# A fused attention, MoE and gated layer in fp32 on one core: attention's small products gathered into one burst per run, and the gated layer's splits planned by when their loads land

## The chip, the cores and the metric

The kernel runs on one core of a Trainium2 chip. The metric is the device time of one execution in microseconds, as the median of several runs. Before the change it is 764.74 us (three runs, 764.42 to 764.76).

## What is computed

Three layers follow each other on 4 sequences of 576 tokens with 512 features, all in float32: attention over a window of 128 tokens with a linear bias per head, a two-layer MoE block with a norm ahead of it, and a gated layer that mixes along the sequence.

```python
scores = scale * np.matmul(q, k.transpose(0, 1, 3, 2))          # 4 x 8 heads, 576 x 576, 64 deep
mask = (rel >= 0) & (rel < window)
scores = np.where(mask, scores + bias[None], -1000000000.0)
attn = np.exp(scores - max); attn = attn / (sum + 1e-09)
x = attn @ v
...
xn = (x - mu) / np.sqrt(var + 1e-06) * g_ln
x = x + np.maximum(xn @ w_ch1, 0.0) @ w_ch2                      # 512 -> 2048 -> 512
...
h = gelu(x @ w_in); u, v = halves of h                           # 512 -> 2 x 512
v_n = (v - mu) / np.sqrt(var + 1e-06) * g_ln
v_s = np.einsum('ts,bsd->btd', w_sg, v_n) + b_sg[None, :, None]  # 576 x 576 along the sequence
out = x + (u * v_s) @ w_out
```

## The kernel before

Every large product is made of three products of float32 values cut into a high and a low part (high x high, high x low, low x high); the parts are made on the chip. A weight comes as 64-bit words by DMA into a buffer `st`, is rounded into a tile `sc` in five steps (Split64, lines 61 to 89: `first` on ACT, L72; `bits` 0 to 3 on DVE, L77, L79, L81, L84; `last` on ACT and POOL, L88 and L89), and gives a high part (as `wvh`) and a low part (`wvl`).

The program has two phases. The first, `phase1`, computes attention and the MoE interleaved. Attention is cut into 40 runs (L252 on): 32 wide ones of two units (128 query tokens of one pair of heads each) and 8 tail runs of one unit. A run goes through these steps: the scores on PE (`scores`, L408, products L444, in tail runs L430); for each of its units, in `unit` (L465), the mask and the reduction on DVE (L477 to L489), the exponential on ACT (L495), the sums and their reciprocals on DVE (L498, L499), the normalising on POOL, ACT or DVE (L503), a pair of transposes on PE (L513, into `tps`), and the copy with its mask (L527 to L533, with POOL's `sel`, L453); then the values on PE (`values`, L563, products L580) and their eviction on ACT (L557 to L560) into the tiles `x`. A group is 256 tokens; `norm(g)` (L594) starts a group's norm when all its runs are evicted: mean (sums on POOL L606, L608, product L611), squares on ACT (L644), their sums on POOL (L649, L651), the variance product (L659), the power on POOL (L665) and the product that spreads rstd (L669). The MoE (`moe`, L704) takes groups and eighths of the weights in a fixed order, `stream`. A step is two halves of 12 products of 128x256 with K = 128: `m1` (L743, into `ps_h`) or `m2` (L754, into `acc`); between them stand the relu on ACT (`hh`, L682) and its low half on DVE (`hl`, L684), and behind a group's last step `evac` (L687) with `et` and `x`.

The order of the instructions is set at build time by a planner (`Sched`). Each step is a generator that yields `Op(engine, estimated ns, priority, need=..., slots=..., token=...)`: it is started on its engine when the tokens in `need` are there and a slot is free, the earliest start first and then the lowest priority. Only the order on each engine comes from this; at run time engines wait for semaphores. An `Op` with engine None waits for its needs and takes no engine. `pts` and `tau` (L292 to L299) turn a unit's number into its priority, so that attention is spread over the MoE's steps; a norm's priority comes from `start` and `LBACK`.

When attention is over, `end_attention` (L801) spawns for each of 21 loads of the gated layer a `flow` (L934): one load on SP into one of four buffers `st` (NS2), and the split steps on ACT, DVE and POOL with three tiles `sc` (NC2). The loads are four pieces each of wv and wu (from `in_wi`), two of x, five of ws and four of wo. `open_1`, `open_2` and `open_3` (L890 to L908) make the room for their results when the MoE's last group is through its steps 7, 5 and 3; `open_2` also loads the bias `bb` and the gain `g` and scales both on DVE (L903). The second phase, `Phase2.run`, is the gated layer: v products (L994), u (L1070), the products along the sequence (L1087) and out (L1115), with the gelu in `ge` (L1026 to L1028) and `vg` (L1031).

## Time and profile before

| | |
|---|---|
| median of three runs | 764.74 us |
| the profiled execution | 765.15 us |
| its span in the profile | 763.4 us |
| mean granted clock of TensorE | 0.991 of full |
| busy: PE / DVE / ACT / POOL | 746.2 / 444.7 / 311.7 / 256.6 us |
| share of the span: PE / DVE / ACT / POOL | 98% / 58% / 41% / 34% |
| products L743 and L754 | 6 groups of 576, 160.7 to 166.7 us busy each |
| moved by DMA | 63.42 MB, 83 GB/s |

The span is what the hardware profiler covers, from the first to the last instruction; the execution's own time is 1.75 us longer. Matmuls overlap in the pipeline, so the durations of single products (0.28 us) add up to more than the time that passes; what a product takes of PE's time is read from the distance of two starts. Line numbers are those of the kernel before, unless a text says "of the changed kernel", where the code stands some 40 lines lower.

### The profile page before, as it was taken

The page shows a single profiled execution, that of the slowest core. Times are in us where ns is not written, and L with a number is a line of the kernel's source. Part 1 is how long each engine was busy: PE and PEld are TensorE (multiplying, and loading weights), DVE is VectorE, ACT ScalarE, POOL GpSimd, SP SyncE. Part 2 cuts the span into 40 slices and gives each one's busy share as a digit, 9 for nine tenths or more (in the row PEclk, how much of TensorE's full clock was granted, in tenths as well). Part 3 has the DMA queues.
Part 4 walks back from the last instruction along what each step waited for, and adds up shares of the span by engine and source line. Part 5 has one row for each costly group of instructions (what it writes and reads, how often), then busy time and mean ns, then how long its engine had stood idle before and what let it go on. Part 6 is the DMA issues. An engine that isn't in the chain of part 4 may idle for free.

```text
span 763.4 us, 15899 instructions
## 1 busy us (share of the span) xinstructions
PE 746.2 (98%) x6270; PEld 692.8 (91%) x6270; DVE 444.7 (58%) x1129; ACT 311.7 (41%) x805; POOL 256.6 (34%) x327
## 2 busy tenths in 40 slices
PE   7999999999999999999999999999899999999998
PEld 3669899999999999999999898999789999999997
DVE  6899888784542532443433335835776646656732
ACT  5896744432432522423423534232354333333410
POOL 2533423432421421412312323217255406317220
PEclk9999999999999999999999999999899999999999
DMA  9654621420121110111111324406130050160002
GB/s 304 203 174 134 179 83 30 131 70 22 59 95 29 49 57 21 44 56 56 29 43 43 79 83 157 142 29 178 38 124 1 32 169 1 47 203 0 2 32 93
DMA packets 51626, 63.42 MB, mean 83 GB/s; under 512 B 10336, under 2 KB 38880, under 8 KB 51552
## 3 DMA queue, kind: packets, MB, share of 16 engines
q1 hardware_dynamic: 51552, 62.41, 26.2%
q8 instruction: 49, 0.80, 0.5%
q14 instruction: 25, 0.20, 0.1%
HBM read 52.96 MB, written 9.44 MB: 82 GB/s over the span
## 4 chain that ended last, share of the span: by engine, by line
PE 90%; POOL 3%; DMA 2%; ACT 2%; DVE 2%; issue 1%; SPq 0%; DVEq 0%; POOLq 0%; ACTq 0%
PE acc L754 25%; PE ps_h L743 24%; PE ps_s L1087 8%; PE ps_u L1070 7%; PE ps_o L1115 7%; PE ps_v L994 6%; PE o L580 4%; PE s L444 3%; PE tps L513 2%; PE ps_ln L659 1%; DMA st<-in_wo 1%; PE ps_ln L602 1%; DMA st<-in_w 1%; POOL x2l L986 1%; PE ps_w L352 1%
## 5 line engine op out<-in xcount | busy, mean ns | idle before, releaser
L754 PE MATMUL acc<-hh,w2h 128*128 128x256 f32 x576 | 166.0, 288 | 2.0 <-ACT hh L682 2.0
L743 PE MATMUL ps_h<-xh,w1h 128*128 128x256 f32 x576 | 166.7, 289 | 0.0
L754 PE MATMUL acc<-hl,w2h 128*128 128x256 f32 x576 | 162.4, 282 | 0.5 <-DVE hl L684 0.5
L754 PE MATMUL acc<-hh,w2l 128*128 128x256 f32 x576 | 162.2, 282 | 0.0
L743 PE MATMUL ps_h<-xh,w1l 128*128 128x256 f32 x576 | 160.7, 279 | 0.0
L743 PE MATMUL ps_h<-xl,w1h 128*128 128x256 f32 x576 | 160.7, 279 | 0.0
L684 DVE SCALAR_TENSOR_TENSOR hl<-ps_h,hh 128x512 fp32r<-128x512 f32 x72 | 49.6, 689 | 141.0 <-ACT hh L682 140.7
L754 PEld LDWEIGHTS acc<-hh,w2h 128*128 128x128 f32 x576 | 110.0, 191 | 6.8 <-ACT hh L682 3.3
L743 PEld LDWEIGHTS ps_h<-xh,w1h 128*128 128x128 f32 x576 | 108.5, 188 | 3.0 <-issue 2.8
L754 PEld LDWEIGHTS acc<-hh,w2l 128*128 128x128 f32 x576 | 110.9, 192 | 0.0
L754 PEld LDWEIGHTS acc<-hl,w2h 128*128 128x128 f32 x576 | 110.1, 191 | 0.8 <-DVE hl L684 0.8
L743 PEld LDWEIGHTS ps_h<-xh,w1l 128*128 128x128 f32 x576 | 108.9, 189 | 0.0
L743 PEld LDWEIGHTS ps_h<-xl,w1h 128*128 128x128 f32 x576 | 108.4, 188 | 0.1
L453 POOL TENSOR_SCALAR_AFFINE_SELECT m<-m 128x256 f32<-128x256 f32 x118 | 53.1, 452 | 154.5 <-ACT m L530 151.2
L682 ACT ACTIVATE hh<-ps_h 128x512 fp32r<-128x512 f32 x72 | 42.8, 594 | 95.5 <-PE ps_h L743 95.5
L495 ACT ACTIVATE t<-t,sm 128x128 f32<-128x128 f32 x144 | 56.2, 393 | 29.5 <-DVE sm L489 29.5
L503 POOL TENSOR_TENSOR t<-t,sm 128x256 f32<-128x256 f32 x52 | 32.9, 634 | 90.0 <-DVE sm L499 70.5
L530 ACT ACTIVATE m<-tps 128x256 f32<-128x256 f32 x62 | 23.7, 382 | 85.2 <-PE tps L513 84.8
L986 POOL TENSOR_TENSOR gl<-gt,gh 128x576 fp32r<-128x576 f32 x16 | 22.9, 1430 | 53.3 <-ACT gh L985 53.3
L72 ACT ACTIVATE sc<-st 128x512 f32<-128x512 f32 (+1 forms) x52 | 30.7, 598 | 24.5 <-DMA st<-in_wo 6.1
L1028 ACT ACTIVATE ge<-ge 128x512 f32<-128x512 f32 (+1 forms) x34 | 22.4, 658 | 37.1 <-DVE ge L1027 37.1
L81 DVE SCALAR_TENSOR_TENSOR sc<-st,sc 128x512 int32<-128x512 int32 (+1 forms) x52 | 36.0, 696 | 0.4
(163 smaller groups left out, 1543.4 us busy)
## 6 DMA issues: line engine op xcount, KB each, us to landing
st<-in_w SPq DMA_DIRECT2D x24, 512.0 KB, 4.0
x2d<-x SPq DMA_DIRECT2D x18, 256.0 KB, 2.0
out<-xr SPq DMA_DIRECT2D x15, 288.0 KB, 2.1
st<-in_w SPq DMA_DIRECT2D x16, 256.0 KB, 2.7
st<-in_wi SPq DMA_DIRECT2D x8, 512.0 KB, 4.0
st<-x2d SPq DMA_DIRECT2D x8, 512.0 KB, 4.8
xr<-x2d SPq DMA_DIRECT2D x8, 512.0 KB, 6.6
rq<-in_q SPq DMA_DIRECT2D x28, 128.0 KB, 2.1
```

The costliest lines, as they stand in the source:

```text
L81: dve.scalar_tensor_tensor(out=xi, in0=self.wh, scalar=-0x40000000, in1=xi, op0=ALU.bitwise_and, op1=ALU.bitwise_or)
L453: pool.affine_select(out=out, in_=in_, pattern=pat, compare_op=ALU.is_ge, fill=0.0, base=-1 if up else 0, channel_multiplier=1 if up else -1)
L495: act.activation(out=t[:, h], in_=t[:, h], func=ACTF.Exp, bias=st[:, h:h + 1], scale=-1.0, accum_out=sums[:, h, 0:1])
L503: pool.tensor_tensor(out=t, in0=t, op=ALU.mult, in1=st[:, 6:8].rearrange("p (h o) -> p h o", o=1).to_broadcast([128, 2, 128]))
L682: act.activation(out=h, in_=ps, func=ACTF.Relu)
L684: dve.scalar_tensor_tensor(out=l, in0=ps, scalar=0.0, in1=h.bitcast(F32), op0=ALU.max, op1=ALU.subtract)
L743: pe.matmul(ps[:, half], w[:, kc, f], m[:, kc], start=kc == 0 and x == 0, stop=kc == 3 and x == 2)
L754: pe.matmul(accs[half][:, d], w[:, f, ds], m[:, k], start=fi and d == 0 and k == 0 and x == 0, stop=la and k == 1 and x == 2, skip_group_c ...
L994: self.nc.tensor.matmul(ps, xs[s][:, kc, c0:c0 + 128], self.wv[m][:, kc], start=kc == 0 and x == 0, stop=kc == 3 and x == 2)
L1070: pe.matmul(ps[:, z, 0:288], wu[s][:, kc, ds], self.x[m][:, kc, 288 * z:288 * z + 288], start=kc == 0 and x == 0, stop=kc == 3 and x == 2)
L1087: pe.matmul(ps[:, z, 0:288], l, r[:, 288 * z:288 * z + 288], start=n == 0, stop=n == len(mm) - 1)
L1115: pe.matmul(ps[:, z, 0:288], wo[s][:, kc, ds], gated[b][m][:, kc, 288 * z:288 * z + 288], start=n == 0, stop=n == 11)
```

## The change

From run KB = 13 on, scores, values and transposes are no longer three kinds of steps of their own. A new generator, `burst(n)`, is one step on PE: the scores of run n+1, the values of run n-1, and the transposes of all units of run n, in this order. It needs the normalised scores of run n (`nm`), the copies of the transposes before (`bl`), and everything that the values of run n-1 wait for (`R`). `scores(n)` returns without doing anything for n > 13, its products having moved into `quarters`; in `unit` the steps for the transposes and the values become steps without an engine that wait for the tokens which the burst sets. So the values of a run come one run later than before. There are 27 bursts (n = 13 to 39); the values of the last run stay a step of their own.

BB = (11, 6) moves the points of `pts`: attention runs four units earlier against the norms, and the last of the points lies 6 halves earlier. In the gated layer's `flow`, the first split step (ACT) now also needs the token `ld2` of its load, which the planner sets at the time when it estimates the load to have landed; the estimate of the first DVE step goes from 1100 to 680 ns, and DVE's steps of a flow count as users of the port that DVE and POOL share in the planner. No operation's shape changes.

```diff
--- before.py
+++ after.py
@@ -54,6 +54,10 @@
 WEARLY = {0: -990, 1: -989, 2: -898, 3: -897}
 NWARM, FILL = 14, 495
 ABANK = 1, 3, 5
+
+
+KB = 13
+BB = 11, 6
 
 NLO = 6
 
@@ -292,7 +296,7 @@
 
     pts = list(PACE)
     for g in range(NF, G):
-        pts.append((71 if g == 8 else 8 * g + 7, start[g] - LBACK[g == 8] - OC - 1))
+        pts.append((71 if g == 8 else 8 * g + BB[0], start[g] - LBACK[g == 8] - OC - 1 - (BB[1] if g == 8 else 0)))
 
     def tau(n):
         for (n0, t0), (n1, t1) in zip(pts, pts[1:]):
@@ -409,6 +413,8 @@
 
 
         p, tail, n = s.p, s.tail, s.n
+        if n > KB:
+            return
         if s.wide:
             z = min(y for _, y, _ in LW if y > p)
             nd = [("wq", z), ("wk", z)]
@@ -417,6 +423,10 @@
         sl = [("a%d" % h, 1, ("cp", n)) for h in range(2)] if n in ABANK else [("s", 1, ("cp", n))]
         yield Op("PE", 420 if tail else 700 if s.i0 == 0 else 810, s.tau, token=("A1", n), slots=sl,
                  need=nd + ([("A1", n - 1)] if n else []))
+        quarters(s)
+
+    def quarters(s):
+        p, tail, n = s.p, s.tail, s.n
         if n in ABANK:
             s.S = [ps_a.tile([128, 2, 256], F32, tag="a%d" % h, name="sa") for h in range(2)]
             s.parts = [(h, s.S[h]) for h in range(2)]
@@ -506,11 +516,14 @@
             for h in range(2):
                 scaled(o.eng, t[:, h], t[:, h], st[:, 6 + h:7 + h])
 
-        yield Op("PE", 220, pri + OB, token=("T", un),
-                 need=["cst", "unf"] + ([("bl", un - 2)] if un >= 2 else []) + ([("T", un - 1)] if un else []))
+        e.t = t
         tp = tps[:, un % 2]
-        for h in range(2):
-            pe.transpose(tp[:, h], t[:, h], ident)
+        if n >= KB:
+            yield Op(None, 0, pri, need=[("T", un)])
+        else:
+            yield Op("PE", 220, pri + OB, token=("T", un),
+                     need=["cst", "unf"] + ([("bl", un - 2)] if un >= 2 else []) + ([("T", un - 1)] if un else []))
+            transposed(e)
         new = ([(i - 1, 0)] if i == s.i0 and i > 0 else []) + [(i, int(not e.last))]
         o = Op(None, 0, pri, slots=[("m%d" % f, NM[f], ("C", n)) for j, f in new], token=("bl", un),
                need=[("bl", un - 1)] if un else [], alt=[("ACT", 275, 740)] + ([] if tail else [("DVE", 670 if i else 335, DVEX)]))
@@ -541,9 +554,13 @@
             nd.append(("wv", s.p))
         else:
             nd.append(("lv", n))
-        yield Op("PE", 500 if tail else 1020 if i > 1 else 760, pri + OC, need=nd, slots=[("o", 1, ("ev", n))],
-                 token=("C", n))
-        values(s)
+        if KB <= n + 1 < len(runs):
+            yield Op(None, 0, pri, need=nd, token=("R", n))
+            yield Op(None, 0, pri, need=[("C", n)])
+        else:
+            yield Op("PE", 500 if tail else 1020 if i > 1 else 760, pri + OC, need=nd, slots=[("o", 1, ("ev", n))],
+                     token=("C", n))
+            values(s)
         x = s.x()
         sl = []
         if x not in xt:
@@ -559,6 +576,31 @@
         else:
             act.activation(out=x[:, p, :], in_=s.O, func=ACTF.Copy)
         yield Op(None, 0, 0, token=("ev", n))
+
+    def transposed(e):
+        for h in range(2):
+            pe.transpose(tps[:, e.un % 2, h], e.t[:, h], ident)
+
+    def burst(s):
+        n = s.n
+        after = runs[n + 1] if n + 1 < len(runs) else None
+        nd = [("nm", e.un) for e in s.units] + [("bl", e.un - 2) for e in s.units if e.un - 2 < s.units[0].un]
+        nd += [("R", n - 1), "cst", "unf"] + ([("A1", n)] if n == KB else [])
+        sl = [("o", 1, ("ev", n - 1))]
+        if after:
+            nd += [("lq", n + 1), ("lk", n + 1)]
+            sl.append(("s", 1, ("cp", n + 1)))
+        dur = 300 + 140 * len(s.units) + (400 if runs[n - 1].tail else 820 if runs[n - 1].i0 else 600)
+        if after:
+            dur += 420 if after.tail else 850 if after.i0 else 600
+        yield Op("PE", dur, (after or s).tau, need=nd, slots=sl)
+        if after:
+            quarters(after)
+        values(runs[n - 1])
+        for e in s.units:
+            transposed(e)
+        for z in [("A1", n + 1), ("C", n - 1)] + [("T", e.un) for e in s.units]:
+            sched.done[z] = sched.free["PE"] + HOPP
 
     def values(s):
 
@@ -817,7 +859,7 @@
     for gen in ([warm(), constants()] + [load_wide(slice(x, y), t) for x, y, t in LW]
                 + [moe(), open_split(), last_quarter(), end_attention()]
                 + [weights(n) for n in range(40)] + [norm(g) for g in range(G)]
-                + [load(s) for s in runs if not s.wide] + [scores(s) for s in runs] + [unit(e) for e in units]):
+                + [load(s) for s in runs if not s.wide] + [scores(s) for s in runs] + [burst(s) for s in runs if s.n >= KB] + [unit(e) for e in units]):
         sched.spawn(gen)
     sched.run("end")
     for p in (ps_a, ps_h, wps.pop(), np_, cp):
@@ -940,14 +982,15 @@
         self.loaded.append(j)
         if j.shape:
             w = int(np.prod(j.shape))
-            yield Op("ACT", 190 + .833 * w, 10 ** 6 + n, need=[("p2", j.name)])
+            yield Op("ACT", 190 + .833 * w, 10 ** 6 + n, need=[("p2", j.name), ("ld2", n)])
             self.loaded.remove(j)
             j.step()
             self.todo[j.label] -= 1
             yield Op("POOL", 60 + 2.3 * w, 10 ** 6 + n, token=("st2", n))
             return
-        for k, (eng, dur) in enumerate((("ACT", 565), ("DVE", 1100), ("DVE", 602), ("DVE", 602), ("ACT", 530))):
-            yield Op(eng, dur, 10 ** 6 + n, need=[("p2", j.name)] if k == 4 else [],
+        for k, (eng, dur) in enumerate((("ACT", 565), ("DVE", 680), ("DVE", 602), ("DVE", 602), ("ACT", 530))):
+            yield Op(eng, dur, 10 ** 6 + n, port=eng == "DVE",
+                     need=[("ld2", n)] if k == 0 else [("p2", j.name)] if k == 4 else [],
                      slots=[("sc2", NC2, ("sc2", n))] if k == 0 else [],
                      token=("st2", n) if k == 3 else None)
             if k == 0:
```

On PE, in the middle of the MoE, where a wide run's unit is transposed; `ps_h<-` is a layer product, `tps<-ident,t` a transpose, `s<-` scores and `o<-` values. Before, a pair of transposes stands alone, and a little later scores and values together:

```order
L743 MATMUL ps_h<-xl,w1h_108 128x256
L743 MATMUL ps_h<-xh,w1l_109 128x256
L513 MATMUL tps<-ident,t 128x128 x2
L743 MATMUL ps_h<-xh,w1h_108 128x256
L743 MATMUL ps_h<-xl,w1h_108 128x256
...
L743 MATMUL ps_h<-xh,w1l_109 128x256
L444 MATMUL s<-rk,rq 64x192 x8
L580 MATMUL o<-m,rv 64x256 x2
L580 MATMUL o<-m,rv 64x128 x2
L754 MATMUL acc<-hh,w2h_110 128x256
```

With the change the same stretch holds one burst:

```order
L785 MATMUL ps_h<-xh,w1l_109 128x256
L454 MATMUL s<-rk,rq 64x64 x2
L454 MATMUL s<-rk,rq 64x128 x2
L454 MATMUL s<-rk,rq 64x192 x4
L622 MATMUL o<-m,rv 64x256 x2
L622 MATMUL o<-m,rv 64x128 x2
L582 MATMUL tps<-ident,t 128x128 x4
L796 MATMUL acc<-hh,w2h_110 128x256
```

The two pairs of a run's transposes have moved behind its neighbours' scores and values, and layer products follow behind the burst.

On POOL, at the last norm of the MoE and the first splits of the gated layer (`sq` the sums of squares, `var` the power, `wvl` a split's low part). Before:

```order
L649 TENSOR_TENSOR sq<-sq 128x512
L89 TENSOR_TENSOR wvl<-sc,wvh 128x512 x2
L651 TENSOR_TENSOR sq<-sq 128x256
L89 TENSOR_TENSOR wvl<-sc,wvh 128x512
L665 TENSOR_TENSOR var<-var,mh 128x2
L89 TENSOR_TENSOR wvl<-sc,wvh 128x512
```

With the change:

```order
L691 TENSOR_TENSOR sq<-sq 128x512
L693 TENSOR_TENSOR sq<-sq 128x256
L93 TENSOR_TENSOR wvl<-sc,wvh 128x512
L707 TENSOR_TENSOR var<-var,mh 128x2
L93 TENSOR_TENSOR wvl<-sc,wvh 128x512 x3
```

Two splits have moved from between the two sums to behind them, one of them behind the power.

On DVE, with the change, where the last group's relu (`hl`) meets the gated layer's splits (`sc`), and at the first v products. `bb` and `g` stand ahead of the last step (L88) of a split, and split steps stand between `et`, `x`, `ge` and `vg`:

```order
L85 SCALAR_TENSOR_TENSOR sc<-st,sc 128x512
L726 SCALAR_TENSOR_TENSOR hl<-ps_h,hh 128x512
L945 TENSOR_SCALAR bb<-bb 128x576
L945 TENSOR_SCALAR g_6797<-g_6797 128x4
L88 SCALAR_TENSOR_TENSOR sc<-st,sc 128x512
L726 SCALAR_TENSOR_TENSOR hl<-ps_h,hh 128x512 x2
...
L735 TENSOR_TENSOR et<-acc,rstd 128x512
L88 SCALAR_TENSOR_TENSOR sc<-st,sc 128x512
L739 TENSOR_TENSOR x<-x,et 128x512
L85 SCALAR_TENSOR_TENSOR sc<-st,sc 128x512
L1070 SCALAR_TENSOR_TENSOR ge<-ge,ps_v 128x512
L88 SCALAR_TENSOR_TENSOR sc<-st,sc 128x512
L1074 SCALAR_TENSOR_TENSOR vg<-ge,ps_v 128x512
```

Before, both steps L81 and L84 of that split stood ahead of `bb`, and no step of a split stood between `ge` and `vg`:

```order
L81 SCALAR_TENSOR_TENSOR sc<-st,sc 128x512
L84 SCALAR_TENSOR_TENSOR sc<-st,sc 128x512
L684 SCALAR_TENSOR_TENSOR hl<-ps_h,hh 128x512
L903 TENSOR_SCALAR bb<-bb 128x576
L903 TENSOR_SCALAR g_6814<-g_6814 128x4
L684 SCALAR_TENSOR_TENSOR hl<-ps_h,hh 128x512
```

The scaling of `bb` has moved from behind a finished split into the middle of one.

## Rows read from the trace of the kernel before

**Rows 1.** Page, chain that ended last, by engine
```profile
PE 90%; POOL 3%; DMA 2%; ACT 2%; DVE 2%; issue 1%; SPq 0%; DVEq 0%; POOLq 0%; ACTq 0%
```

**Rows 2.** Timeline of PE, a lone pair of transposes: start, us, what
```profile
152.11 0.28 PE L754 MATMUL acc<-hh,w2l 128*128 128x256 f32 x1
152.23 0.38 PE L513 MATMUL tps<-ident,t 128*128 128x128 f32 x2
...
152.57 0.28 PE L754 MATMUL acc<-hl,w2h 128*128 128x256 f32 x1
```

**Rows 3.** Timeline of PE, the scores of a run alone
```profile
207.26 0.28 PE L743 MATMUL ps_h<-xh,w1l 128*128 128x256 f32 x1
...
208.40 0.28 PE L754 MATMUL acc<-hl,w2h 128*128 128x256 f32 x1
```

**Rows 4.** Timeline of PE, the values of a run alone
```profile
87.03 0.28 PE L754 MATMUL acc<-hh,w2l 128*128 128x256 f32 x1
...
88.26 0.28 PE L743 MATMUL ps_h<-xl,w1h 128*128 128x256 f32 x1
```

**Rows 5.** Timeline of PE, scores and values in one break
```profile
221.31 0.28 PE L743 MATMUL ps_h<-xh,w1l 128*128 128x256 f32 x1
221.52 0.77 PE L444 MATMUL s<-rk,rq 64*64 64x64 f32 x16
...
223.24 0.28 PE L754 MATMUL acc<-hl,w2h 128*128 128x256 f32 x1
```

**Rows 6.** Timeline of PE, scores, values and a pair of transposes in one break
```profile
75.52 0.28 PE L754 MATMUL acc<-hh,w2l 128*128 128x256 f32 x1
...
77.24 0.44 PE L513 MATMUL tps<-ident,t 128*128 128x128 f32 x2
...
77.63 0.28 PE L754 MATMUL acc<-hl,w2h 128*128 128x256 f32 x1
```

**Rows 7.** The chain in order of time, 300 to 315 us: start, us, what
```profile
302.37 1.42 PE ps_h L743 x12
...
311.83 2.72 PE acc L754 x24
```

**Rows 8.** Timelines of POOL and PE, first long wait: [idle before <-releaser]
```profile
473.95 3.17 POOL L89 TENSOR_TENSOR wvl<-sc,wvh 128x512 fp32r<-128x512 f32 x2
477.08 0.90 POOL L651 TENSOR_TENSOR sq<-sq 128x256 f32<-128x256 f32 x1
...
478.04 0.61 PE L659 MATMUL ps_ln<-ones,sq 128*128 128x1 f32 x4 [2.29 <-POOL sq L651]
```

**Rows 9.** Three stretches: us, busy PE, PEld, DVE, ACT, POOL, granted clock, DMA, GB/s
```profile
478.50:482.90 4.40, 4.40 (x26) 4.40 (x26) 4.34 (x9) 2.39 (x4) 1.87 (x2) 0.61 0.36 119
538.20:543.30 5.10, 5.04 (x23) 5.04 (x24) 4.65 (x6) 0.94 (x2) 2.19 (x2) 0.50 0.00 0
551.90:556.20 4.30, 3.00 (x13) 2.18 (x12) 3.34 (x8) 2.00 (x5) 0.55 (x1) 1.00 0.77 253
```

**Rows 10.** Timeline of PE at the second long wait
```profile
537.31 0.43 PE L754 MATMUL acc<-hh,w2h 128*128 128x256 f32 x1 [1.99 <-ACT hh L682]
538.26 0.58 PE L754 MATMUL acc<-hl,w2h 128*128 128x256 f32 x1 [0.52 <-DVE hl L684]
```

**Rows 11.** Timeline of DVE, and the chain, before the second long wait
```profile
526.00 0.85 DVE L903 TENSOR_SCALAR bb<-bb 128x576 f32<-128x576 f32 x1 [2.41 <-DMA bb<-in_bsg]
...
528.18 6.56 DMA st<-in_wo
```

**Rows 12.** Timeline of PE, third v product of the gated layer
```profile
553.60 0.50 PE L994 MATMUL ps_v<-wvh,x2h 128*128 128x512 f32 x1 [1.30 <-DVE vg L1031]
```

**Rows 13.** Page, costliest groups: busy, mean ns, idle before, releaser
```profile
L81 DVE SCALAR_TENSOR_TENSOR sc<-st,sc 128x512 int32<-128x512 int32 (+1 forms) x52 | 36.0, 696 | 0.4
```

**Rows 14.** Timelines of PE and POOL, one tail unit from scores to normalised scores
```profile
438.36 0.56 PE L430 MATMUL s<-rk,rq 64*64 64x192 f32 x8
...
441.06 0.61 POOL L503 TENSOR_TENSOR t<-t,sm 128x256 f32<-128x256 f32 x1 [3.91 <-DVE sm L499]
```

## The prediction

> **What bounds the kernel now.** I read the page first, then the chain of waits, the timeline of PE at every place where the stream of layer products is interrupted, and last the busy times by stretch. Products with 256 columns of the MoE layer (L743, L754) are called layer products here. The chain is 90% PE [rows 1]: nearly everything counts that shortens PE's own stream, and nothing that only shortens another engine, unless PE waits for it. The reader is to see three kinds of lost PE time. The first is the breaks: each time attention puts a few small products into the stream, the stream needs some time beyond its own. The second is the pace of the layer products behind a break. The third is two long waits near the end of the MoE, each with a stretch of half clock behind it.
>
> A break is priced from the start of the last layer product ahead of it to the start of the second one behind it, less two steps of 0.113 us. A lone pair of transposes: 152.57 - 152.11 = 0.46, so 0.23 us [rows 2]. The scores of a run alone: 1.14 - 0.23 = 0.91 [rows 3]. Its values alone: 1.23 - 0.23 = 1.00 [rows 4]. Scores and values in one break: 1.93 - 0.23 = 1.70, which is 0.21 less than apart [rows 5]. Scores, values and a pair of transposes together: 2.11 - 0.23 = 1.88, so the pair costs 0.17 there instead of 0.23 [rows 6].
>
> The pace is the odd reading. The chain shows 12 layer products in 1.42 us, 0.118 each, and elsewhere 24 in 2.72 us, 0.113 each [rows 7]. Over the chain from 100 to 476 us about 1,450 of some 2,640 layer products go at the slower pace: 1,450 x 0.0047 = 6.8 us. The pace changes only at a break. Of 41 lone pairs of transposes 39 left the slow pace behind them; breaks of scores with values, and all 12 pairs that stood behind other small products, left the fast one.
>
> The first long wait: POOL does two splits (L89) of 3.17 us together, and only then the second sum of squares that the last norm needs, so PE idles 2.29 us ahead of the variance products [rows 8]. In the 4.40 us behind it the granted clock is 0.61 [rows 9], a mixture of the two levels: 4.40 x 0.39 = 1.7 us lost. The second: PE idles 1.99 us for the relu on ACT and 0.52 for its low half on DVE [rows 10], and 5.10 us then run at 0.50, which is 1.2 GHz [rows 9]: 2.55 lost. What made relu late is DVE: the scaling of bb stood in its queue and waited 2.41 us for its load [rows 11], and everything behind it slid.
>
> **The change, part by part.**
>
> A, the breaks. From product 252 of the stream on, the changed order has 48 breaks where there were 86. Of the 40 runs 12 already had scores and values joined; 6 more are joined now: 6 x 0.21 = 1.2 us. In 19 wide runs the pairs of transposes move from breaks of their own to the end of a burst, 0.23 to 0.17: with two pairs in a row, some of them already behind other products, I take 0.07 a run, 1.3 us. The tail runs and norms give some 0.2. Together -2.7; from 0 (the small products cost the same wherever they stand) to -4.0 (all 38 saved breaks at 0.11).
>
> B, the pace. In the changed order lone pairs are gone from run 13 on, every burst ends in transposes behind values, and the breaks that stay alone are a norm's mean, variance and rstd. I count the layer products behind such a break up to the next burst: 96 in each of four groups, some 130 in the last, about 520, and some 260 before the first burst as now. That makes 780 slow products, 3.7 us, where there were 6.8: **-3.1**. The ends are -6.8 (all fast) and +4.7 (a burst leaves the slow pace behind it, then all behind the first burst are slow, some 2,190, and the 260 ahead of it: 2,450 x 0.0047 = 11.5, less 6.8). I take the first value, since the nearest case [rows 6] left the fast pace behind its transposes.
> The Trainium skill, page "TensorE: Matmul & The Clock Gate", section "Back-to-back issue gap", gives one isolated gap for a size, N/2.4 + 2.5 ns, by which I estimate 109 ns for 256 columns at full clock, and no second value. By it B would be 0. This case's trace shows two, 118 and 113, so the measurement decides, and the rule stands as a rival below.
>
> C, the first long wait. POOL's order is now both sums of squares, then a split, then the power: the split of 3.17 us no longer stands ahead of the second sum [rows 8]. That removes 2.29 of idle time and, if the clock then stays up, 1.7 more: -4.0. The upper bound is 0, when the squares come late anyway. Attention ends 96 layer products earlier against the end of the stream, 10.9 us, so the loads of the gated layer start earlier and the splits with them; that speaks for the gain.
>
> D, the tail. The ACT step that starts a split now waits in the planner for its load, so relu is planned ahead of splits whose data is not there. That should remove the second wait: 1.99 + 0.52 + 2.55 = 5.1 us [rows 9, 10]. Against it: on SP bb and g now go ahead of four ws loads, and on DVE the last step of wu's last split (L88 of the changed kernel) stands behind bb and g. That split's buffer comes free later, and the wo loads queue behind it; one of those took 6.56 us [rows 11]. Three split steps of wo then stand between DVE's et, x, ge and vg, and the third v product waits for vg, by 1.30 us already [rows 12]. Three steps of 0.70 [rows 13] make that 3.4, so +2.1. Both earlier waits of about 2 us had half clock behind them while the 1.30 us did not (a clock of 1.00 in the third stretch [rows 9]), so I add 2.1, between 1.7 and 2.55. Net -5.1 + 4.2 = **-0.9**. Ends: -5.1, when nothing of the new wait comes, and +3, when the second wait stays in half and the new one comes whole.
>
> Nothing of the arithmetic is added or removed; masks, exponentials and evictions keep their counts and lie under PE's stream, and if that cover went the third rival below would be the price.
>
> Sum: -2.7 - 3.1 - 4.0 - 0.9 = -10.7. The profiled execution took 765.15 us, 0.41 above the median of the runs, 764.74. So 765.15 - 10.7 = 754.45 there, **754.0** against the median.
>
> **The rivals.**
> 1. A clean tail: the new wait at the third v product doesn't come, since its splits are DVE work that could fall in gaps. D is -5.1: 749.8. For it speaks that the loads start 10.9 us earlier. 15%.
> 2. Bursts leave the slow pace: B is +4.7 instead of -3.1: 761.8. For it: every burst ends in transposes, and lone transposes leave the slow pace. Against it: the 12 pairs behind other products [rows 6]. 13%.
> 3. The pace doesn't follow the breaks at all (one gap for one size, the rule cited above): B is 0, 757.1. Against it: 39 of 41. 10%.
> 4. The first wait stays, because the squares come late behind the splits on ACT and DVE: C is 0, 758.0. 7%.
> 5. On the slower side: a burst needs everything at once, the values' masks of the run before and the normalised scores of this one; when any is late, PE stands still with all three products behind it. The slack between two bursts is 96 products, 10.9 us, in wide runs and 36 to 48, 4.1 to 5.4 us, in the tail runs. In the trace a tail unit takes 441.67 - 438.36 = 3.3 us from its scores to its normalised scores [rows 14], so a wait has about 0.8 us of room there and much more in the wide runs. There are 27 bursts, so the gain of 10.7 us is gone from a wait of 10.7 / 27 = 0.40 us per burst on; at 0.5 us each the time is 754.0 + 13.5 = 767.5. 5%.
>
> **How the numbers follow.** My forecast has 50%, the rivals 50% together. The likeliest case gives 754.0 us. The range goes from 746.5 (the clean tail with part A at its end and a little more of B, 749.8 - 1.3 - 2) to 761.5 (which holds rivals 3 and 4 and ends just short of rival 2). A measurement of this kernel tells about 0.2% from no change, 1.5 us. Slower by more than that needs rival 5: 0.05. Within it, rival 2 with the first wait staying as well, or weak waits at the bursts: 0.04. Faster: 0.91.
>
> **What would show it.** Right: lone pairs of transposes are missing after run 13; a whole burst with four transposes costs about 2.1 us beyond two steps; layer products in the chain go at 0.113 behind bursts and at 0.118 behind a norm's lone products; the wait ahead of the variance products is below 1 us and the clock behind it near 1.00; no wait for relu at the last step. Wrong in B: 0.118 behind bursts. Wrong in D: no idle time at the third v product, or a wait of over 4 us there. Wrong altogether: PE idle ahead of bursts, released by POOL, ACT or DVE from the normalising or the masks.

## The result, and the profile after

The changed kernel takes 755.37 us in the median of four runs (752.81 to 756.14), against 764.58 us for the kernel before in the same comparison: a ratio of 0.9866, with a 95% interval of 0.9848 to 0.9885. The forecast was 754.0, in a range of 746.5 to 761.5, and faster. The profiled execution took 752.81 us, with a span of 750.8.

The chain of the changed kernel is PE's even more than before [rows 1]:

```profile
PE 93%; DVE 2%; DMA 1%; ACT 1%; POOL 1%; issue 1%; SPq 0%; DVEq 0%; POOLq 0%; ACTq 0%
```

Of PE's waits between 440 and 600 us, four before, one is left (the wait, us in total, times, longest):

```profile
PE ps_v L1037 <- DVE vg L1074: 3.2, 1, 3.2
```

The stream of layer products is the same 3,456 in both kernels, so the start of the same product can be compared in two traces. This table gives the us between the starts of layer products number 252, 2,900, 3,000 and 3,455 on PE's timeline, then to the end of PE's last product. Product 252 stands before the first burst. Up to it PE's order is the same in both kernels, but for one pair of transposes that the changed kernel has just ahead of it.

| kernel, profiled execution | 252 to 2,900 | to 3,000 | to 3,455 | to the end | sum | slow products, 100 to 476 us |
|---|---|---|---|---|---|---|
| before | 378.22 | 16.59 | 60.37 | 210.49 | 665.67 | 1,419 |
| changed | 373.68 | 11.33 | 54.42 | 213.66 | 653.10 | 1,034 |
| difference | -4.5 | -5.3 | -5.9 | +3.2 | -12.6 | -385 |

"Slow" are distances between two layer products of 0.1155 to 0.121 us. In the first column the changed kernel has already done the last norm's variance and rstd products (0.46 us each, beyond the product's step), which the kernel before does in the second. So breaks and pace together gained 4.54 + 0.92 = 5.5 us, and the first long wait 5.26 - 0.92 = 4.3.

One burst on PE's timeline, from the last layer product ahead of it to the second behind it: 279.00 - 276.46 - 0.23 = 2.31 us, with 12 records of values (a record is one product in the trace). Between the kinds nothing waits:

```profile
276.46 0.28 PE L785 MATMUL ps_h<-xh,w1l 128*128 128x256 f32 x1
276.67 0.77 PE L454 MATMUL s<-rk,rq 64*64 64x64 f32 x16
...
278.39 0.65 PE L582 MATMUL tps<-ident,t 128*128 128x128 f32 x4
278.80 0.36 PE L796 MATMUL acc<-hh,w2h 128*128 128x256 f32 x1
279.00 0.28 PE L796 MATMUL acc<-hl,w2h 128*128 128x256 f32 x1
```

The pace, in the chain from 211 to 227 us: a burst with 24 layer products behind it in 2.83 us, 0.118 each, and the next one, of the same kinds, with 24 in 2.74, 0.114 each. Before, it was 0.118 or 0.113 too [rows 7]:

```profile
211.35 0.70 PE s L454 x12
212.06 0.80 PE o L622 x8
212.86 0.59 PE tps L582 x4
213.45 2.83 PE ps_h L785 x24
...
221.93 0.81 PE s L454 x16
222.74 0.80 PE o L622 x8
223.54 0.59 PE tps L582 x4
224.13 2.74 PE acc L796 x24
```

POOL at the last norm, and PE's variance products, which before had waited 2.29 us behind two splits [rows 8]: both sums of squares are done at 457.4, the split comes 3 us later, and PE's row at 458.85 has no idle time ahead of it:

```profile
455.11 1.37 POOL L691 TENSOR_TENSOR sq<-sq 128x512 f32<-128x512 f32 x1 [5.36 <-ACT sq L686]
456.56 0.81 POOL L693 TENSOR_TENSOR sq<-sq 128x256 f32<-128x256 f32 x1
460.31 1.29 POOL L93 TENSOR_TENSOR wvl<-sc,wvh 128x512 fp32r<-128x512 f32 x1 [2.94 <-ACT wvh L92]
...
458.85 0.39 PE L701 MATMUL ps_ln<-ones,sq 128*128 128x1 f32 x3
```

The granted clock behind it and in the tail, where it was 0.61 and 0.50 before [rows 9] (us, busy PE, PEld, DVE, ACT, POOL, clock, DMA, GB/s):

```profile
463.00:468.00 5.00, 5.00 (x46) 5.00 (x46) 3.73 (x8) 2.67 (x5) 1.29 (x1) 1.00 0.36 108
538.00:543.00 5.00, 3.32 (x9) 2.62 (x10) 4.71 (x10) 2.73 (x6) 1.41 (x3) 0.75 0.96 297
543.00:548.00 5.00, 5.00 (x25) 4.23 (x24) 1.83 (x5) 2.12 (x4) 4.63 (x5) 0.91 0.55 202
```

The new wait, on DVE and then on PE. bb waits 3.98 us for its load (2.41 before [rows 11]) with the split's last step behind it; a split step stands between ge and vg, and PE waits 3.25 us for vg, where it was 1.30 [rows 12]:

```profile
515.64 0.46 DVE L945 TENSOR_SCALAR bb<-bb 128x576 f32<-128x576 f32 x1 [3.98 <-DMA bb<-in_bsg]
516.09 0.69 DVE L88 SCALAR_TENSOR_TENSOR sc<-st,sc 128x512 int32<-128x512 int32 x1
...
537.94 1.09 DVE L88 SCALAR_TENSOR_TENSOR sc<-st,sc 128x512 int32<-128x512 int32 x1
538.95 0.68 DVE L1074 SCALAR_TENSOR_TENSOR vg<-ge,ps_v 128x512 f32<-128x512 f32 x1
...
539.68 0.50 PE L1037 MATMUL ps_v<-wvh,x2h 128*128 128x512 f32 x1 [3.25 <-DVE vg L1074]
```

### The profile page after: what moved, and what is told of

It is laid out like the page before. It is cut to its first block, busy times and chain, and to the rows that moved or that the text cites. A ratio compares the mean times of both kernels' runs of the same rounds, so it can differ in the third digit from the quotient of the medians.

```text
span 750.8 us, 15850 instructions
## 1 busy us (share of the span) xinstructions
PE 736.4 (98%) x6270; PEld 685.9 (91%) x6270; DVE 448.3 (60%) x1149; ACT 308.5 (41%) x795; POOL 245.8 (33%) x307
## 4 chain that ended last, share of the span: by engine, by line
PE 93%; DVE 2%; DMA 1%; ACT 1%; POOL 1%; issue 1%; SPq 0%; DVEq 0%; POOLq 0%; ACTq 0%
PE ps_h L785 26%; PE acc L796 25%; PE ps_s L1130 8%; PE ps_u L1113 7%; PE ps_o L1158 7%; PE ps_v L1037 6%; PE o L622 5%; PE tps L582 3%; PE s L454 3%; PE ps_ln L701 1%; DMA st<-in_w 1%; PE ps_ln L644 1%; DMA st<-in_wo 1%; PE ps_w L356 1%; PE s L440 1%
## 5 line engine op out<-in xcount | busy, mean ns | idle before, releaser
L796 PE MATMUL acc<-hh,w2h 128*128 128x256 f32 x576 | 163.6, 284 | 0.0
L785 PE MATMUL ps_h<-xh,w1h 128*128 128x256 f32 x576 | 163.0, 283 | 0.0
L796 PE MATMUL acc<-hl,w2h 128*128 128x256 f32 x576 | 160.1, 278 | 0.0
L796 PE MATMUL acc<-hh,w2l 128*128 128x256 f32 x576 | 160.0, 278 | 0.0
L796 PEld LDWEIGHTS acc<-hl,w2h 128*128 128x128 f32 x576 | 108.4, 188 | 0.2
L796 PEld LDWEIGHTS acc<-hh,w2l 128*128 128x128 f32 x576 | 108.3, 188 | 0.0
L463 POOL TENSOR_SCALAR_AFFINE_SELECT m<-m 128x256 f32<-128x256 f32 x100 | 44.7, 452 | 143.7 <-ACT m L543 141.6
L622 PE MATMUL o<-m,rv 128*64 128x128 f32 (+3 forms) x416 | 34.7, 296 | 0.3 <-POOL m L463 0.3
```

Source lines behind the costliest of these rows:

```text
L463: pool.affine_select(out=out, in_=in_, pattern=pat, compare_op=ALU.is_ge, fill=0.0, base=-1 if up else 0, channel_multiplier=1 if up else -1)
L622: pe.matmul(s.O[64 * h:64 * h + 64, oc:oc + w], v, s.M[m][0:k, h, mc:mc + w], start=x == 0, stop=x == len(mm) - 1, skip_group_check=True)
L785: pe.matmul(ps[:, half], w[:, kc, f], m[:, kc], start=kc == 0 and x == 0, stop=kc == 3 and x == 2)
L796: pe.matmul(accs[half][:, d], w[:, f, ds], m[:, k], start=fi and d == 0 and k == 0 and x == 0, stop=la and k == 1 and x == 2, skip_group_c ...
```

## The experiments

"Sum" means the sum of the table above, from layer product 252 to the end.

**The changed kernel again**, with no edit.

> The changed kernel once more, to see what its spread is made of: its four runs lie between 752.81 and 756.14 us, ten times the spread of the kernel before, and the profiled one is the fastest of them. Theory: the spread is the half clock behind the wait at the third v product (3.25 us of idle time, then stretches at 0.75 and 0.91, some 1.6 us lost); the slower executions lose more there, so a profile of a slower one shows a granted clock below 0.75 in the 5 us behind that wait and the same stream up to it. Rival: the pace of the layer products differs from execution to execution; then the time of the last layer product differs by 1 us or more, and the tail is the same. Time expected 752.5 to 756.5 either way.

Measured: 754.91 us in the median of five runs (753.02 to 755.53). The profiled one took 755.53, and its sum is 653.33: within 0.2 us of the first profile, with 1,042 slow products. So neither theory nor rival holds: nearly all of the 2.7 us lies ahead of product 252, which starts at 96.53 us here and at 93.94 in the first profile (94.07 before). Two windows of the opening, first profile and then this one, with the window behind the tail's wait last:

```profile
10.00:20.00 10.00, 7.61 (x69) 4.67 (x70) 8.91 (x51) 9.47 (x44) 5.07 (x10) 0.83 1.05 382
20.00:30.00 10.00, 9.20 (x76) 5.54 (x75) 8.70 (x40) 8.44 (x32) 6.03 (x10) 1.00 0.64 186
```

```profile
10.00:20.00 10.00, 6.63 (x54) 3.77 (x54) 8.63 (x51) 8.34 (x35) 3.79 (x8) 0.70 1.02 375
20.00:30.00 10.00, 9.04 (x82) 5.00 (x79) 8.01 (x40) 7.88 (x30) 5.31 (x10) 0.96 0.41 134
541.00:546.00 5.00, 3.47 (x9) 2.77 (x10) 4.71 (x9) 2.78 (x6) 1.42 (x3) 0.71 0.92 292
```

In this execution the opening had the half clock for longer (0.70 against 0.83, then 0.96 against 1.00). Why it does in one execution and not in another these runs don't show. It concerns neither the bursts nor the flow, so from here on sums are compared, and medians beside them.

**Bursts in the order transposes, scores, values.** The edit, in `burst`:

```diff
+        for e in s.units:
+            transposed(e)
         if after:
             quarters(after)
         values(runs[n - 1])
-        for e in s.units:
-            transposed(e)
```

> The burst in the order transposes, scores, values, so that values end it. Theory: the last kind of small product in a break sets the pace behind it; lone values left the fast pace in each case of both traces, bursts that end in transposes left the slow pace 7 times of 27 in the changed kernel. Then all layer products behind a burst go at 0.113: some 370 fewer at 0.118, 1.7 us faster than the changed kernel, and the trace shows no burst with 0.118 behind it. Rival: the pace depends on where in its cycle PE stands when the break comes, whatever kind ends it; then some bursts leave 0.118 still, about as many as now, and the time stays within 1 us.

Measured: 753.58 us (752.91 to 754.09), sum 653.60, against 653.10 and 653.33. The pace half of the theory came true: 724 slow products instead of 1,034, and 17 of the 18 wide bursts leave 0.113. But three of the tail bursts still leave 0.118 though values end them, and the gain of 1.3 us in pace (5.94 to 4.66 us up to product 2,900, counted as what the steps between breaks take beyond 0.113 us each) is paid by the breaks: each burst costs 0.05 us more, 27 times, 1.3 us.

**Bursts in the order scores, transposes, values.** The edit moves the loop over `transposed(e)` between the two others.

> The burst in the order scores, transposes, values: values end it too, but scores stand first and the transposes lie between kinds. Theory (the last kind sets the pace): as with transposes first, 1.7 us faster than the changed kernel, no burst with 0.118 behind it. Rival (the place in PE's cycle): a mixed pattern, another one than with transposes first, time within 1 us of the changed kernel.

Measured: 758.85 us (757.65 to 760.67), sum 658.07, 5 us more. Slow products 1,202: of ten wide bursts with 12 records of values five leave 0.118, and five 0.113, though values end all of them. "The last kind decides" falls. The trace of the kernel before has such cases as well: three lone breaks of 12 values, at 115, 141 and 168 us, left 0.118, which the expectations had overlooked. And the burst itself got dearer by 0.19 us, which neither side had expected.

**Bursts in the order values, transposes, scores.**

> The burst in the order values, transposes, scores, the changed kernel otherwise. The three orders so far cost, per wide burst with 8 records of values, 2.15 us (scores, values, transposes), 2.20 (transposes, scores, values) and 2.35 (scores, transposes, values) on average, with 1,040, 724 and 1,202 slow layer products from 100 to 476 us. Theory: a change of kind costs by its two kinds, and transposes between scores and values are the dear ones: 2.3 to 2.4 us per burst here too, 5 us slower than the changed kernel. Rival: what is dear is values behind transposes; then about 2.2 us, and the time within 1.5 us. For the pace, theory: scores at the end leave the fast pace behind (the one lone case in the changed trace did), below 800 slow ones; rival: as many as in the changed kernel.

Measured: 757.82 us (757.12 to 759.25), sum 657.14. Both theories hold: the price is that of the other order with transposes in the middle, and with scores at the end 693 products are slow, the fewest; all 18 wide bursts leave the fast pace, though behind one of them two sets of 24 products are slow later on (more on these at the end). The four orders, by PE's timelines (price of a burst as in the prediction, mean over the wide bursts of a kind; the last column is the sum of the prices of all breaks from product 252 to 2,900):

| order | 8 records of values | 12 records | slow products | all breaks, us |
|---|---|---|---|---|
| scores, values, transposes (the change) | 2.15 | 2.38 | 1,034 | 68.5 |
| transposes, scores, values | 2.20 | 2.43 | 724 | 69.8 |
| values, transposes, scores | 2.35 | 2.58 | 693 | 73.5 |
| scores, transposes, values | 2.35 | 2.58 | 1,202 | 73.6 |

In the kernel before all breaks there come to 71.5 us. Two of the four orders that were run would have made the breaks dearer than they were. The one that the change takes is the cheapest in breaks and not the best in pace; by the sum it is level with transposes first.

**bb and g scaled late.** The loads stay in `open_2`; the scaling moves to just ahead of the products along the sequence.

```diff
-        for x in (self.bb, self.g2):
-            self.nc.vector.tensor_scalar(x, x, 0.5, None, ALU.mult)
...
+        for x in (self.bb, self.g2):
+            dve.tensor_scalar(x, x, 0.5, None, ALU.mult)
         self.need("ws")
```

> The changed kernel with the scaling of bb and g on DVE moved from open_2 to just ahead of the gated layer's products along the sequence; the loads stay where they are, the planned order of the other instructions too. Theory: DVE's wait of 3.98 us for the load of bb, with the last step of wu's split behind it, is what makes the wo loads late and puts wo's split steps between et, x, ge and vg; without it those steps are done some 3 to 4 us earlier, and the wait at the third v product falls from 3.25 us to 1.3 or less with no half clock behind it: 2.5 to 3.5 us faster than the changed kernel, and a smaller spread. Rival: the wo loads are late by the room for wo, which the MoE's last steps give free (open_3), and by the order on DVE alone; then the wait stays near 3.2 us and the time within 1 us.

Measured: 751.00 us (750.82 to 751.20), sum 651.01, 2.1 us less than the changed kernel, and 3.9 in the medians. Of the 4.5 us between this profiled execution and that of the changed kernel again, 2.3 lie ahead of product 252 (94.27 and 96.53 us), so only the 2.1 are put down to the edit. DVE's row (the split's last step, now at 511.92 instead of 516.09), PE's wait and the window behind it:

```profile
511.92 0.68 DVE L88 SCALAR_TENSOR_TENSOR sc<-st,sc 128x512 int32<-128x512 int32 x1
...
PE ps_v L1035 <- DVE vg L1072: 2.3, 1, 2.3
...
538.00:543.00 5.00, 3.90 (x16) 2.90 (x17) 4.67 (x10) 2.78 (x7) 1.60 (x2) 1.00 0.95 311
```

The wait is 2.3 us, not 1.3 or less, and no half clock follows: the clock is 1.00 where it was 0.75. So bb is a part of the cause and not all of it. This version beats both kernels.

**The flow alone**: the kernel before, with the diff's last part only.

> The kernel before with the change of the gated layer's flow alone: no bursts, attention's points as before. Its order on POOL has both sums of squares of the last norm ahead of the splits, and on DVE split steps of wo between et, x, ge and vg, as in the changed kernel. Theory: the two long waits went by this part alone, and the new one at the third v product came by it. Counted from layer product 252 on in the two traces, C was -5.3 and D -2.7, so about -8.0 against the kernel before, some 757, with 1,400 or so slow layer products from 100 to 476 us as before. Rival: the first wait went because attention ends earlier with the bursts; then PE waits some 2 us for the sum of squares here, and the time is about 762.

Measured: 758.44 us (757.77 to 761.49), sum 658.26, so -7.4. PE's waits behind the opening:

```profile
PE ps_v L995 <- DVE vg L1032: 3.0, 1, 3.0
PE ps_r L669 <- POOL var L665: 0.7, 1, 0.7
```

The theory holds: no wait at the variance products, 0.7 us at rstd instead, and the new wait at the third v product is there without any burst. Which of the three edits in `flow` does it (the token, the estimate or the port) was not run apart. By stages, against before: -0.2 up to product 2,900, -3.1 to 3,000, -5.9 to 3,455, +1.8 to the end.

**The bursts and points alone**: the changed kernel with `flow` as before.

> The changed kernel with the gated layer's flow as before: bursts and attention's new points alone. POOL's order keeps the two splits between the sums of squares. Theory: the breaks and the pace are worth 4.6 us together, which is what the changed trace gains up to layer product 2,850, and both long waits stay as they are: about -4.6 against the kernel before, 760. Rival: since attention ends 96 layer products earlier, the splits have been done by the time of the last norm and the first wait goes too; then about -9, 755 to 756, and no idle time of PE at the variance products.

Measured: 763.00 us (761.21 to 765.50, twelve runs), a ratio of 0.9969 [0.9957, 0.9981]; sum 664.10, so only -1.6. The theory's place was right, and the size was not: the wait at the variance products is longer than before, 2.91 us, and 6 us at 0.50 follow it, 3 us lost.

```profile
458.74 1.30 POOL L691 TENSOR_TENSOR sq<-sq 128x512 f32<-128x512 f32 x1 [8.06 <-ACT sq L686]
459.99 3.15 POOL L93 TENSOR_TENSOR wvl<-sc,wvh 128x512 fp32r<-128x512 f32 x2
463.09 0.91 POOL L693 TENSOR_TENSOR sq<-sq 128x256 f32<-128x256 f32 x1
...
464.06 0.58 PE L701 MATMUL ps_ln<-ones,sq 128*128 128x1 f32 x2 [2.91 <-POOL sq L693]
...
464.00:470.00 6.00, 5.95 (x28) 5.95 (x29) 5.89 (x12) 2.37 (x4) 2.41 (x3) 0.50 0.33 94
```

Up to product 3,000 this kernel took 392.8 us and the changed one 385.0: with bursts the flow is worth 7.8 us there, without them 3.3. By these profiles the two parts are worth more together (-12.6) than one by one (-1.6 and -7.4), but that isn't shown: the medians differ from the kernel before by 2.6 and 7.2 us for the parts and by 9.2 and 10.1 for the whole. The profiled execution here is 1.5 us above its median. Up to product 2,760, ahead of the last norm's wait, it is the changed kernel's to 0.01 us: both take 356.05 us from product 252, and the kernel before 359.38. That part of the gain doesn't need the flow.

**Attention's points as before**: BB = (7, 0) in the changed kernel.

> The changed kernel with attention's points as before, BB = (7, 0): attention runs four units later against the norms, bursts and flow as changed. Theory: the points matter little, the breaks are the same and POOL's order at the last norm is the same; within 1.5 us of the changed kernel. Rival: without the four units of lead a norm, or a burst, waits for the attention in front of it: PE idles ahead of a norm's mean in one or more groups, at 1 us or more each, 3 us slower or more.

Measured: 775.13 us (772.41 to 778.51), slower than the kernel before, a ratio of 1.0141 [1.0119, 1.0163]; sum 672.56, 19.5 us above the changed kernel. The rival holds, with more lost than it said. At 208, 268, 327 and 387 us a norm comes with no layer products left to put between its mean, a burst and its variance; the first of the four:

```profile
209.01 0.60 PE L653 MATMUL ps_ln<-sum,ones 128*128 128x256 f32 x2
209.54 0.78 PE L454 MATMUL s<-rk,rq 64*64 64x64 f32 x16
210.24 0.87 PE L622 MATMUL o<-m,rv 128*64 128x256 f32 x8
211.04 0.85 PE L582 MATMUL tps<-ident,t 128*128 128x128 f32 x4
214.78 0.61 PE L701 MATMUL ps_ln<-ones,sq 128*128 128x1 f32 x4 [2.89 <-POOL sq L693]
...
PE ps_ln L701 <- POOL sq L693: 10.9, 4, 2.9
```

So 10.9 of the 19.5 us are idle time of PE. Behind each of the four waits layer products went at 0.213 us for a while; the granted clock of the whole execution is 0.982, where the changed kernel's is 0.995. So the lower clock is a large part of the rest.

The burst puts a run's values one run later, so the group's norm has its inputs later; four units of lead in the points make up for that. What the points alone do to the kernel before was not run.

**bb late, and the split steps between the first two v products recorded behind the third.** The edit is `play(V(0)[:2], 0)`.

> The changed kernel with bb and g scaled late, and without the split steps that were recorded between the first two v products' ge and vg (they come behind the third v product). With bb late alone PE still waited 2.3 us at the third v product. Theory: what is left of that wait is DVE's own queue, of which the split step L88 between ge and vg took 1.08 us and the one ahead of ge 0.68; without the first the wait falls to about 1.2 us, 1.1 us faster than with bb late alone, some 750. Rival: vg is late by et and x, which wait for the last layer products, and the wait stays within 0.3 us of 2.3.

Measured: 752.16 us (751.78 to 752.44), sum 651.82, and the wait was 3.2 us. Not conclusive: in this execution a load of wo took 5.25 us that took 3.53 in the trace with bb late alone, and the splits behind it, with DVE's whole sequence, came 1.2 us later. What can be read is that without the step between ge and vg DVE idled 0.69 us there for the tanh on ACT, so of the 1.08 us at most 0.4 were to be had.

**The last two splits of wo out of the planner**, with bb late. In `flow`, behind the load:

```diff
+        if j.label == "wo" and j.at[0] > 1:
+            return
```

> The changed kernel with bb and g scaled late, and the splits of the last two pieces of wo taken out of the planner: they are recorded behind the third v product, between the later chunks. With bb late alone the wait at the third v product was 2.3 us, and ACT's square of the first v stood behind a woh that waited 4.26 us for DVE. Theory: those split steps are the rest of the wait (two DVE steps of 0.68 and one of 1.08 ahead of vg, and ACT's wait): it falls to 1 us or less, 1.3 us faster than with bb late alone, with a clock of 1.00 behind it. Rival, after the run that only moved steps behind the first v and found 3.2 us: vg waits for et and x, so for the last layer products, and the wait stays at 2 us or more; or the wo splits, now late, are missed later, by a wait at the first out products, and the time is that of bb late alone or more.

Measured: 754.23 us (751.89 to 754.42), sum 653.80. Both halves came: the wait at the third v product fell to 0.7 us, and another of 2.5 took its place at the products along the sequence, behind u on DVE.

```profile
PE ps_s L1130 <- DVE u L1074: 2.5, 1, 2.5
PE ps_v L1037 <- DVE vg L1074: 0.7, 1, 0.7
```

**The same, with those steps recorded still later**, none among the v and u chunks (`play(..., 0)` twice).

> As the kernel with the last two splits of wo taken out of the planner, but their steps recorded between the first products along the sequence, behind all v and u chunks. In that run the wait at the third v product fell to 0.7 us, as the theory said, and 2.5 us came back at the products along the sequence, which waited for u on DVE. Theory: DVE has less to do there than among the v and u chunks, so that the 2.5 us go and nothing takes their place: the part behind the last layer products takes some 210 us, where it took 211.57 with bb late alone and 214.36, and the time is 749.5 to 750. Rival: the first out products and the loads of the next sequence are late then, since two buffers are held longer; the wait moves there, and the time is 751 or more.

Measured: 755.84 us (755.00 to 756.39), sum 655.29. The rival holds: the next sequence's x pieces now come late, and v waits for their split.

```profile
PE ps_v L1037 <- POOL x2l L1029: 2.8, 1, 2.8
```

Two more waits there are 0.9 and 0.7 us. Three places were tried for the same DVE steps of wo, and each time a wait came up. With bb late alone it was the smallest.

**Bursts from run 9 on**, KB = 9, with bb late.

> Bursts from run 9 on in place of 13, with bb and g scaled late. Theory: the price of a break holds there too: four more runs lose their lone pairs of transposes, 4 times 2 pairs at 0.06 and two joins at 0.2, some 0.9 us, and the pace gains up to 1 us, so 1 to 2 us faster than with bb late alone. Rival: between 60 and 100 us attention itself is what the layer products wait for; values that come a run later make the norms late, as with the old points, and the time is 2 us slower or more with idle PE ahead of a norm.

Measured: 754.27 us (753.15 to 755.86), 3.3 slower in the median than with bb late alone. The rival holds: layer product 2,000 starts 2.45 us later than with bb late alone (339.72 and 337.27), and product 971 by as much already. One break at 106 us now holds a norm's mean, its variance and a burst and costs 7.7 us, with 0.8 us of it idle PE behind the norm's squares; the other kernels pay for most of these products too, but apart. And there are more slow products, 1,252 for 1,039. How the 2.45 us divide between the two was not worked out.

## Why the prediction was right, point by point

The time and its sign were right, and the sum was near: -12.6 by the two profiles, where -10.7 was forecast. The medians differ by 9.2 and, in the second comparison, by 10.1: the first profiled execution of the changed kernel is the fastest of its four, and the second, 2.7 us longer, differs from it in the opening alone.

- **A, the breaks: -2.7 forecast, -3.9 measured** (71.5 to 68.5 us, and 0.9 for the two norm products that moved ahead of product 2,900). Mis-sized, within the bounds. The prices of single breaks held, and "0.07 a run" was right: joined scores and values cost 1.75 us with 8 records of values and 2.00 with 12, on average, and two lone pairs 0.47, which is some 0.06 and 0.09 more than the wide bursts' 2.15 and 2.38. The term that was low is "some 0.2" for the tail runs and norms. In the tail 8 scores alone cost 433.14 - 432.22 - 0.23 = 0.69 us, 16 values alone 0.96 and a pair 0.23; in one burst of the changed kernel they cost 402.73 - 400.88 - 0.23 = 1.62, so 0.26 less. Over the eight tail runs, some of which had joined a part of this before, that is some 1.1 us, an estimate from the prices of these breaks. What the prediction didn't see is that the order inside the burst decides the sign of A: with transposes between the two other kinds A would have been a loss of 1.1 us (73.5 - 0.9 - 71.5). The tail's breaks before, then with the change:

```profile
432.22 0.28 PE L743 MATMUL ps_h<-xh,w1l 128*128 128x256 f32 x1
...
433.14 0.28 PE L754 MATMUL acc<-hl,w2h 128*128 128x256 f32 x1
...
440.39 0.28 PE L743 MATMUL ps_h<-xh,w1l 128*128 128x256 f32 x1
...
441.58 0.28 PE L754 MATMUL acc<-hl,w2h 128*128 128x256 f32 x1
```

```profile
400.88 0.28 PE L785 MATMUL ps_h<-xh,w1l 128*128 128x256 f32 x1
...
402.73 0.28 PE L796 MATMUL acc<-hl,w2h 128*128 128x256 f32 x1
```

- **B, the pace: -3.1 forecast, -1.5 measured** (the steps between breaks take 7.46 us beyond 0.113 each before, and 5.94 with the change, up to product 2,900). What failed is the step from "every burst ends in transposes behind values" to the fast pace behind all of them. Of the 8 wide bursts with 8 records of values 5 left 0.118, of the 10 with 12 records none, of the 9 bursts of the tail 2: rival 2 came for 7 of 27, and 1,034 products were slow where 780 had been worked out.

  Of the 12 cases on which the step rested, 8 stood behind a norm's products. The nearest [rows 6] had the same 16 scores and 8 values and one pair where a burst has two, and it did leave the fast pace. One reading was wrong as well: not all breaks of scores with values left the fast pace before, since the one at 193.00 us left 0.118. That the last kind decides is refuted by the order scores, transposes, values.

  Rival 3 falls as it was put, with no effect of the breaks at all: the orders move the count of slow products between 693 and 1,202 without changing one layer product, and five more executions with the change's own order up to there took 373.68 us to product 2,900 like the first. But "the pace changes only at a break" isn't true either, as the last section shows. What sets the pace stays open.

  The Trainium skill, page "TensorE: Matmul & The Clock Gate", section "Back-to-back issue gap", names the gap from which I had estimated 109 ns as that of an isolated product, and says that in a stream of weight loads and products the two together set the spacing. So no run here tests that figure, and the prediction was wrong to set the 113 and 118 ns, which every trace here shows side by side in such a stream, against it.
- A and B together: -5.8 forecast, and -5.5 measured. That the sum was right is luck: A gave 1.2 us more than forecast and B 1.6 less.
- **C, the first long wait: -4.0 forecast, -4.3 measured**, by the mechanism named: in the kernel with the flow alone POOL's order has changed, and the wait is gone; with the bursts alone the order is the old one, and the wait is there. Rival 4 falls.
- **D, the tail: -0.9 forecast, -2.8 measured** (-5.95 + 3.17). Each step came: the relu waits went, bb made wu's last step wait on DVE, three split steps of wo stood between et, x, ge and vg, and the third v product waited 3.25 us where 3.4 was worked out. What was too large is the half clock behind it: 2.1 forecast, and 1.2 by difference (3.17 less the 1.95 by which the wait grew). What was too small is the gain of the old waits, 5.9 for 5.1. Rival 1, the clean tail, didn't come by itself; moving bb's scaling got 2.1 us of it.
- **Rival 5** did not come, but a relative did as soon as the points were left as they were: 19.5 us, at four places. The prediction used the points only as an argument for C, and costed them at nothing. Without them the same bursts and flow made the kernel slower than before.

## What to carry to other kernels

A step that is gathered with others waits for the latest of them and delivers late for the earliest: before gathering, ask whose input comes later by it (here the norm's), and give the lead back in the same change. Small products of several kinds in one break are priced as a sequence, by what stands next to what, and not as a sum. And a step that waits for nothing can still sit in a queue behind one that waits for a load: scale a constant where it is needed, not where it is loaded.

## What the runs showed that was not expected

- In the four orders that were run, a pair of neighbours goes with the price of a burst: scores next to values cost 2.15 to 2.20 us per burst, transposes between them 2.35, for the same 28 records. The two other orders were not run.
- Two paces of the same layer products, 0.113 and 0.118 us, mostly last from one break to the next. In the changed kernel's trace from 100 us on, lone products for a norm's mean or variance left 0.118 each time (6 and 5 of them); over the whole trace lone rstd products turned one pace into the other, seven times of seven.
- Three sets of 24 layer products (numbers 648, 696 and 936 on) are slow in every trace, whatever breaks stand around them. In the changed kernel no break stands at either end of them; the products ahead and behind go at 0.113 or 0.114. During the third set the profile shows no work of DVE, ACT, POOL and the DMA engines, and the clock is 1.00, so other engines' work isn't needed for the slow pace. The chain, then the stretch (us, busy PE, PEld, DVE, ACT, POOL, clock, DMA, GB/s):

```profile
182.75 2.72 PE acc L796 x24
185.47 2.83 PE ps_h L785 x24
```

```profile
185.30:188.00 2.70, 2.70 (x25) 2.70 (x24) 0.00 (x0) 0.00 (x0) 0.00 (x0) 1.00 0.00 0
```

- The opening, ahead of the first burst, differed by 2.6 us between two executions of the same kernel, with a granted clock of 0.83 and 0.70 from 10 to 20 us: more than several of the effects that were measured here. Only times from a fixed product on could tell them apart.
